# Batch 0's intermediates stored and loaded in three parts of eight instead of two of twelve

## The chip, the cores and the metric

The kernel runs on one core of one Trainium2 chip. The metric is the device time of one execution in microseconds (us). The engines are named as the profile names them: PE is TensorE's matrix multiply and PEld its weight load, DVE is VectorE, ACT is ScalarE, POOL is GpSimd, and SP is SyncE, which here does nothing but issue DMAs. One KB is 1024 bytes; the profile's GB/s are bytes per nanosecond.

## What is computed

Two batches of 3008 tokens with 256 features go through a spectral layer (Fourier transform along the tokens, a complex 256x256 product, a soft threshold, the inverse transform), and the result goes through two MLPs of width 2048. The change touches the spectral layer alone.

```python
X = np.fft.rfft(x, axis=1)                    # x: 2 x 3008 x 256
Yr = Xr @ w_r - Xi @ w_i + b_r
Yi = Xr @ w_i + Xi @ w_r + b_i
Y  = soft_threshold(Yr, 0.01) + 1j * soft_threshold(Yi, 0.01)
y  = np.fft.irfft(Y, n=3008, axis=1)
y  = prelu(y @ w_in1, alpha) @ w_out1         # 256 -> 2048 -> 256
out = g(y @ w_in2) @ w_out2                   # quadratic gate, 256 -> 2048 -> 256
```

## The kernel before

The transform over 3008 tokens is split as 47 x 64. **F1**, the function `f1(g)` (L400 to L421), does the 47-point part for one of 16 groups `g` (0 to 7 are batch 0, 8 to 15 batch 1): four matmuls a half from `xs[g]`, one eviction on ACT and one on DVE into a tile `ae`. Its result has 24 frequencies `k`, each with a real and an imaginary row, along the partitions. The 64-point part needs them along the free side, so the data goes through DRAM: `store_a(k, h)` (L388) writes part `h` of the frequencies of two groups from `ae` to `a_dr[h]`, and `load_a(b, k, n)` (L378) reads frequencies `k` to `k+n-1` of batch `b` back into `a_sb[b]`. Batch 0 has two parts of `N1 = 12` frequencies, batch 1 one part of 24. The columns of the constant `c_f1` put the frequencies of the two parts on every second partition, so that one store takes 48 rows of 8 x 1 KB, 384 KB in all.

**F2** (`f2_parts`, L465) is the 64-point part of one *item*, two frequencies of one batch: item 0 takes frequencies 0 and 1 of batch 0, item 4 takes 8 and 9, item 6 takes 12 and 13, item 12 is the first of batch 1. Its tile on PE is `psf`; it reads `a_sb` (tile `a`) and a table `m`. `mix_sum` and `mix` do the complex product against `wm` (tiles `psk`, `ri`), and `i1` the first inverse part against a table `n` (tile `psi`). The item loop (L733) runs at step `j` F2 of item `j+2`, then `mix_sum` of `j+1`, `mix` of `j`, `i1` of `j-2`. After the spectral layer come the MLPs, which hold PE for the rest of the run.

The order of the work is written out by hand: every engine runs its instructions in the order in which the Python lines stand. The loads of `x` come in `X_CHUNKS`; `X_FULL` names the groups that are loaded as 128 full rows, with their zero rows, in one DMA of 512 KB. The other groups are loaded as 96 rows in two DMAs (64 rows and 32 rows), and their zero rows are written by the `memset` loop at L361, on DVE for groups 3, 5, 7, 9 and on POOL for the rest. A table (L434) says which DMAs SP issues behind which F1 group ("s0" is the store of groups 0 and 1's first part, "w0" the load of `w_r`, "x12" the load of groups 12 and 13, "b0" the bias):

```python
early_loads = {-1: "x0 x1 x2 x4 b0 x6 x8", 1: "s0 x10", 3: "s1", 5: "s2", 7: "s3 w0 w1 x12"}
```

Behind these, SP issues from L452 on: half of table m0, frequencies 0 to 3, x14, the other half of m0, frequencies 4 to 7, n0, frequencies 8 to 11, m1, and the stores of the second part. After F1 of the last groups come two stores of batch 1, the load of frequencies 12 to 23 and tables n1 and m2. A DMA's semaphore is one of eight in turn, so SP also waits, before an issue, for the DMA that was issued eight before it. Between F1 of groups 11 and 12 PE does one bias matmul and four matmuls on a tile of zeros (`warm`, L535) whose result nobody uses.

Of the kernel before, what the change touches and what calls it, by code (L numbers as in the profile page):

```python
# [8 lines left out]
F32 = mybir.dt.float32  # L9
# [7 lines left out]
B, S, D = 2, 3008, 256  # L17
R1, R2 = 47, 64
NK = 24
# [9 lines left out]
X_CHUNKS = [(0, 1), (1, 1), (2, 2), (4, 2), (6, 2), (8, 2), (10, 2), (12, 2), (14, 2)]  # L29
X_FULL = (0, 1)  # L30
N1 = 12
PAIRS = [(0, 512), (1024, 512), (2048, 480)]


def fourier_constants():
# [6 lines left out]
    cs = np.stack([np.cos(a), -np.sin(a)], axis=1)  # L42
    c = np.zeros((2, 64, 4, 64))
    rows = np.array([2 * i if i < 32 else 4 * (i - 32) + 1 for i in range(R1)])
    first, second = (cs[:, :, k].reshape(R1, -1) for k in (slice(0, N1), slice(N1, NK)))
    c[:, rows, 0, 16::2], c[:, rows, 0, 17::2] = first, second
    c[:, rows, 1, 0:48:2], c[:, rows, 1, 1:49:2] = first, second
    c[:, rows, 2, 16:] = c[:, rows, 3, :48] = cs.reshape(R1, 48)
    c = c.reshape(128, 256)

    g = np.zeros((2, 64, 64))
    g[:, 0:96 // 2:2, :R1] = np.cos(a).T
    g[:, 1:96 // 2:2, :R1] = -np.sin(a).T
    g = g.reshape(128, 64)
# [3 lines left out]
    m = np.zeros((NT, 2, 2, NK, 2, R2))  # L58
# [17 lines left out]
    m = m.reshape(8, 2, 2, 2, 2, NK, 2, R2).transpose(0, 1, 4, 2, 3, 5, 6, 7)  # L76
    w = w.reshape(2, R2, NK // 2, 2, 128).transpose(3, 1, 2, 0, 4)
    f = np.float32
# [23 lines left out]
def spectral_mlp_kernel(ctx: ExitStack, tc: tile.TileContext, x, w_r, w_i, bias, c_f1, c_f2,  # L102
# [7 lines left out]
    dram = ctx.enter_context(tc.tile_pool(name="dram", bufs=1, space=DRAM))  # L110
# [31 lines left out]

    a_dr = [dram.tile([8, 4, 2, k, D], F32, name=f"a_dr{k}") for k in (2 * N1, 2 * NK - 2 * N1, 2 * NK)]
    v_dr = [dram.tile([96, NT, D], F32, name=f"v_dr{b}") for b in range(B)]
# [215 lines left out]
    V.memset(warm, 0.0)  # L360
    for g in range(2, 16):  # L361
        (V if g in (3, 5, 7, 9) else G).memset(xs[g], 0.0)
# [15 lines left out]
    def load_a(b, k, n):  # L378
        if a_sb[b] is None:
            a_sb[b] = block(f"a{b}", [128, NK, D], F32, f"a_{b}")  # L380
        h = 2 if b else int(k >= N1)
        src = a_dr[h].rearrange("j w q (z k) f -> (j w q z) k f", z=2)
        k0 = k - N1 * (h == 1)
        nc.sync.dma_start(a_sb[b][:, k:k + n, :], src[:, k0:k0 + n, :])

    A_ROWS = (slice(16, 112, 2), slice(17, 113, 2), slice(16, 112))

    def store_a(k, h, z=None):  # L388
        j = 2 * k % 8
        src, groups = (aes[k], slice(j, j + 2)) if z is None else (aes[k, z], slice(j + z, j + z + 1))  # L390
        dst = a_dr[h][groups].rearrange("j w q i f -> (q i) (j w) f")
        nc.sync.dma_start(dst, src[A_ROWS[h]].rearrange("p g s r f -> p (g s r) f"))

# [39 lines left out]
    wm_src = (w_r, w_i)  # L433
    early_loads = {-1: "x0 x1 x2 x4 b0 x6 x8", 1: "s0 x10", 3: "s1", 5: "s2", 7: "s3 w0 w1 x12"}  # L434

# [21 lines left out]
    load_mn(0, n_t, c_i1)  # L457
    load_a(0, 8, 4)
    load_mn(1, m_t, c_f2)
    for k in range(4):  # L460
        store_a(k, 1)
    conv = conversions(0, list(range(NF)))
    items = [(b, i) for b in range(B) for i in range(NK // 2)]
# [70 lines left out]
    V.tensor_copy(b_t, ri[0])  # L534
    for _ in range(4):  # L535
        T.matmul(ri[1].rearrange("p z e -> p (z e)"), warm[:, 0:128], warm, start=True, stop=True)
# [159 lines left out]
    n = len(items)  # L696
# [28 lines left out]
    for z in range(2):  # L725
        store_a(5, 2, z)
    load_a(0, 12, 12)
    load_mn(1, n_t, c_i1)
    load_mn(2, m_t, c_f2)
    for _ in range(2):  # L730
        next(conv)
    store_a(6, 2)
    for j in range(n):  # L733
# [9 lines left out]
        if j == 3:  # L743
            store_a(7, 2)
            for z in range(2):
                store_a(4, 2, z)
        if j == 6:
# [283 lines left out]
    for i in range(len(seq)):  # L1031
        l, c, f = seq[i]
# [108 lines left out]
```

## Time and profile before

| | before |
|---|---|
| median of 3 runs | 1088.78 us (1088.38 to 1089.55) |
| the profiled execution's own time | 1089.89 us |
| its span, first to last instruction | 1088.1 us |
| PE busy | 1075.9 us, 99% |
| DVE busy | 901.5 us, 83% |
| ACT busy | 815.2 us, 75% |
| moved by DMA | 101.54 MB |

The span is one execution; its own time is 1.8 us more than the span, for what lies around the first and the last instruction. The stretches, waits and timelines used below count from the span's start. A share of busy time is an average over stages: the first 40 us, in which the DMA engines are the busiest part of the core, differ from all that follows, where PE is.

### The profile page before, as it was taken

What the parts mean: (1) busy time and instruction counts of PE and PEld (TensorE: products, weight loads), DVE (VectorE), ACT (ScalarE), POOL (GpSimd) and SP (SyncE); (2) the same over time, 40 slices, a digit from 0 to 9 for tenths busy, and PEclk for the clock granted to TensorE, in tenths of its full rate; (3) what the DMA queues carried; (4) which work ended last, traced back from release to release, by engine and by line L of the source; (5) the groups of instructions that cost most, each with busy time, mean ns of one, the idle gap of its engine ahead of it and who ended that gap; (6) DMA issues with size and microseconds to landing.
All of it is one profiled execution on the core that took longest, in us unless ns stands there. A gap on an engine that the chain in (4) does not pass through costs nothing.

```text
span 1088.1 us, 17038 instructions
## 1 busy us (share of the span) xinstructions
PE 1075.9 (99%) x6376; PEld 940.1 (86%) x6376; DVE 901.5 (83%) x1578; ACT 815.2 (75%) x1497; POOL 45.9 (4%) x46
## 2 busy tenths in 40 slices
PE   7999999999999999999999999999999999999998
PEld 2888888888888998888899988888899888888897
DVE  6788678888879879989989887877878878878876
ACT  4677776656767768888888777778778878877876
POOL 3045400000000000000000000000000000000000
PEclk9999999999999999999999999999999999999999
DMA  9996672001322413315245810010100000100100
GB/s 342 363 316 182 171 162 72 20 20 78 112 105 107 146 43 132 117 60 173 64 134 229 309 40 1 1 39 1 37 3 1 37 1 1 39 1 1 39 1 37
DMA packets 46901, 101.54 MB, mean 93 GB/s; under 512 B 4290, under 2 KB 25922, under 8 KB 45635
## 3 DMA queue, kind: packets, MB, share of 16 engines
q1 hardware_dynamic: 46530, 100.08, 27.3%
q8 instruction: 50, 0.82, 0.3%
q10 hardware_dynamic: 288, 0.39, 0.1%
q14 instruction: 33, 0.26, 0.1%
HBM read 64.92 MB, written 35.52 MB: 92 GB/s over the span
## 4 chain that ended last, share of the span: by engine, by line
PE 83%; ACT 2%; DVE 2%; issue 1%; DVEq 0%; ACTq 0%
PE pq L124 11%; PE pq L125 11%; PE pq L126 11%; PE seeded L124 4%; PE seeded L125 4%; PE seeded L126 4%; PE psh L124 4%; PE pso L124 4%; PE psh L125 4%; PE psh L126 4%; PE pso L125 4%; PE pso L126 4%; PE psA L124 3%; PE psA L125 3%; PE psA L126 3%; PE psC L126 3%
## 5 line engine op out<-in xcount | busy, mean ns | idle before, releaser
L124 PE MATMUL pq<-gh,w 128*128 128x512 f32 (+1 forms) x576 | 216.5, 376 | 0.1
L125 PE MATMUL pq<-gl,w 128*128 128x512 f32 (+1 forms) x576 | 215.9, 375 | 0.1
L126 PE MATMUL pq<-gh,w 128*128 128x512 f32 (+1 forms) x576 | 215.8, 375 | 0.0
L893 ACT ACTIVATE gh<-ta 128x512 fp32r<-128x512 f32 (+1 forms) x144 | 88.1, 620 | 90.8 <-DVE ta L890 84.9
L677 ACT ACTIVATE ta<-psh,slopes 128x512 f32<-128x512 f32 (+1 forms) x96 | 65.2, 679 | 78.7 <-DVE ta L679 42.2
L124 PEld LDWEIGHTS pq<-gh,w 128*128 128x128 f32 x576 | 108.8, 189 | 14.8 <-ACT yt L922 2.1
L125 PEld LDWEIGHTS pq<-gl,w 128*128 128x128 f32 x576 | 108.9, 189 | 13.2 <-DVE gl L896 0.5
L126 PEld LDWEIGHTS pq<-gh,w 128*128 128x128 f32 x576 | 108.9, 189 | 12.9
L896 DVE TENSOR_TENSOR gl<-tb,gh 128x512 fp32r<-128x512 f32 (+1 forms) x96 | 65.3, 681 | 58.5 <-ACT gh L893 58.3
L896 DVE TENSOR_TENSOR gl<-ta,gh 128x512 fp32r<-128x512 f32 (+1 forms) x144 | 97.3, 676 | 2.5 <-ACT gh L893 0.8
L121 DVE TENSOR_TENSOR gl<-ta,gh 128x512 fp32r<-128x512 f32 (+1 forms) x96 | 65.2, 679 | 36.7 <-ACT gh L118 36.4
L981 DVE TENSOR_TENSOR h<-psC,s 128x512 f32<-128x512 f32 (+1 forms) x72 | 48.8, 678 | 40.8 <-PE psC L126 33.1
L124 PE MATMUL psh<-mxh,w 128*128 128x512 f32 (+1 forms) x192 | 72.2, 376 | 0.1
L124 PE MATMUL pso<-gh,w 128*128 128x512 f32 (+1 forms) x192 | 72.3, 377 | 0.0
L125 PE MATMUL pso<-gl,w 128*128 128x512 f32 (+1 forms) x192 | 71.9, 375 | 0.0
L126 PE MATMUL pso<-gh,w 128*128 128x512 f32 (+1 forms) x192 | 71.9, 375 | 0.0
L126 PE MATMUL psh<-mxh,w 128*128 128x512 f32 (+1 forms) x192 | 71.9, 375 | 0.0
L125 PE MATMUL psh<-mxl,w 128*128 128x512 f32 (+1 forms) x192 | 71.9, 375 | 0.0
L679 DVE SCALAR_TENSOR_TENSOR ta<-psh,slopes,ta 128x512 f32<-128x512 f32 (+1 forms) x96 | 70.5, 734 | 0.0
L890 DVE SCALAR_TENSOR_TENSOR tb<-tb,h 128x512 f32<-128x512 f32 (+1 forms) x96 | 60.7, 673 | 0.0
L882 ACT ACTIVATE ta<-ta 128x512 f32<-128x512 f32 (+1 forms) x96 | 59.2, 617 | 1.5
L893 ACT ACTIVATE gh<-tb 128x512 fp32r<-128x512 f32 (+1 forms) x96 | 59.3, 617 | 0.0
(169 smaller groups left out, 2626.9 us busy)
## 6 DMA issues: line engine op xcount, KB each, us to landing
s<-kept SPq DMA_DIRECT2D x32, 512.0 KB, 4.5
u<-in_w_in SPq DMA_DIRECT2D x32, 256.0 KB, 3.0
u<-in_w_out SPq DMA_DIRECT2D x32, 256.0 KB, 3.2
kept<-sh SPq DMA_DIRECT2D x16, 512.0 KB, 3.0
kept<-wh SPq DMA_DIRECT2D x16, 512.0 KB, 2.8
w<-kept SPq DMA_DIRECT2D x16, 512.0 KB, 5.7
v_dr<-ve SPq DMA_DIRECT2D x12, 512.0 KB, 4.6
v<-v_dr SPq DMA_DIRECT2D x32, 192.0 KB, 5.1
```

The lines of the kernel that those rows point to most:

```text
L121: V.tensor_tensor(lo, src, hi.bitcast(F32), op=ALU.subtract)
L124: T.matmul(ps, wl, xh, start=start, stop=False, skip_group_check=chained)
L125: T.matmul(ps, wh, xl, start=False, stop=False, skip_group_check=chained)
L126: T.matmul(ps, wh, xh, start=False, stop=stop, skip_group_check=chained)
L677: A.activation(ta, ps, AF.Copy, scale=slope[:, f:f + 1])
L679: V.scalar_tensor_tensor(ta, ps, sign[:, f:f + 1], ta, op0=ALU.mult, op1=ALU.max)
L882: A.activation(self.t, self.t, AF.Square)
L890: V.scalar_tensor_tensor(self.t, self.t, 1.0, self.h, op0=ALU.min, op1=ALU.max)
L893: A.activation(halves(self.gh, self.m), like_halves(self.t, self.m), AF.Copy)
L896: V.tensor_tensor(halves(self.gl, self.m), like_halves(self.t, self.m), halves(self.gh, self.m).bitcast(F32), op=ALU.subtract)
L981: V.tensor_tensor(blk.h, ps[x], ps[y_], op=ALU.add)
```

## The change

The 24 frequencies of batch 0 go to DRAM in three parts of `NS = 8` instead of two of 12, each on every third partition; a store takes 32 rows and 256 KB. The stores of the first part stay where they were; those of the second stand behind m1 as before, and then comes a load of frequencies 8 to 15 (1024 KB) in place of the load of 8 to 11 (512 KB) that stood ahead of m1. The stores of the third part follow that load, and the load of 16 to 23 (1024 KB) takes the place of that of 12 to 23 (1536 KB). Group 1 of `x` is loaded as 96 rows in two DMAs, and POOL writes its zero rows ahead of the other groups'. The loads of `w_r` and `w_i` move ahead of the stores s1 to s3. PE does three `warm` matmuls instead of four. Indices of batch 1's part go from 2 to 3, and nothing else of it changes.

```diff
-X_FULL = (0, 1)
-N1 = 12
+X_FULL = (0,)
+NS = 8
...
-    first, second = (cs[:, :, k].reshape(R1, -1) for k in (slice(0, N1), slice(N1, NK)))
-    c[:, rows, 0, 16::2], c[:, rows, 0, 17::2] = first, second
-    c[:, rows, 1, 0:48:2], c[:, rows, 1, 1:49:2] = first, second
+    for m in range(3):
+        part = cs[:, :, NS * m:NS * m + NS].reshape(R1, -1)
+        c[:, rows, 0, 16 + m::3] = c[:, rows, 1, m:48:3] = part
...
-    for g in range(2, 16):
+    for g in range(1, 16):
         (V if g in (3, 5, 7, 9) else G).memset(xs[g], 0.0)
...
-    A_ROWS = (slice(16, 112, 2), slice(17, 113, 2), slice(16, 112))
+    A_ROWS = (slice(16, 112, 3), slice(17, 112, 3), slice(18, 112, 3), slice(16, 112))
...
-    early_loads = {-1: "x0 x1 x2 x4 b0 x6 x8", 1: "s0 x10", 3: "s1", 5: "s2", 7: "s3 w0 w1 x12"}
+    early_loads = {-1: "x0 x1 x2 x4 b0 x6 x8", 1: "s0 x10 w0 w1", 3: "s1", 5: "s2", 7: "s3 x12"}
...
     load_mn(0, n_t, c_i1)
-    load_a(0, 8, 4)
     load_mn(1, m_t, c_f2)
     for k in range(4):
         store_a(k, 1)
+    load_a(0, 8, 8)
+    for k in range(4):
+        store_a(k, 2)
...
-    for _ in range(4):
+    for _ in range(3):
         T.matmul(ri[1].rearrange("p z e -> p (z e)"), warm[:, 0:128], warm, start=True, stop=True)
...
-    load_a(0, 12, 12)
+    load_a(0, 16, 8)
```

On SP, from the store s1 to the load of x14, the order before is:

```order
L392 DMA a_dr24_71<-ae1_145 48x8x256
L392 DMA a_dr24_71<-ae2_163 48x8x256
L392 DMA a_dr24_71<-ae3_181 48x8x256
L444 DMA wm32_0_108<-in_w_r 128x512
L444 DMA wm32_1_109<-in_w_i 128x512
L375 DMA x_b_81<-in_x 64x2048
L375 DMA x_b_81<-in_x 32x2048
```

and in the changed kernel, where `a_dr0` is the first part:

```order
L444 DMA wm32_0_110<-in_w_r 128x512
L444 DMA wm32_1_111<-in_w_i 128x512
L392 DMA a_dr0_71<-ae1_150 32x8x256
L392 DMA a_dr0_71<-ae2_168 32x8x256
L392 DMA a_dr0_71<-ae3_186 32x8x256
L375 DMA x_b_82<-in_x 64x2048
L375 DMA x_b_82<-in_x 32x2048
```

The two weight loads pass the three stores, which carry 32 rows instead of 48, and the load x12 stays behind all five.

Further down on SP, from table n0 to the big load, the order before is (`a_dr24_72` is the second part, `a_0` is `a_sb[0]`, `a_dr48` batch 1's part):

```order
L397 DMA n0_105<-in_c_i1 128x1024
L384 DMA a_0_204<-a_dr24_71 128x1024
L397 DMA m1_103<-in_c_f2 128x1024
L392 DMA a_dr24_72<-ae0_125 48x8x256
L392 DMA a_dr24_72<-ae1_145 48x8x256
L392 DMA a_dr24_72<-ae2_163 48x8x256
L392 DMA a_dr24_72<-ae3_181 48x8x256
L392 DMA a_dr48_73<-ae10_240 96x4x256
L392 DMA a_dr48_73<-ae11_249 96x4x256
L384 DMA a_0_204<-a_dr24_72 128x3072
```

and in the changed kernel (`a_dr1` is the second part, `a_dr2` the third):

```order
L397 DMA n0_107<-in_c_i1 128x1024
L397 DMA m1_105<-in_c_f2 128x1024
L392 DMA a_dr1_72<-ae0_128 32x8x256
L392 DMA a_dr1_72<-ae1_150 32x8x256
L392 DMA a_dr1_72<-ae2_168 32x8x256
L392 DMA a_dr1_72<-ae3_186 32x8x256
L384 DMA a_0_207<-a_dr1_72 128x2048
L392 DMA a_dr2_73<-ae0_128 32x8x256
L392 DMA a_dr2_73<-ae1_150 32x8x256
L392 DMA a_dr2_73<-ae2_168 32x8x256
L392 DMA a_dr2_73<-ae3_186 32x8x256
```

The load that holds frequencies 8 to 11, and with them items 4 and 5, now stands directly behind the four stores that it reads, where before it stood behind n0 and read a part that had been stored long before.

## Rows read from the trace of the kernel before

**Rows 1.** The page's first part: busy time and share of each engine.
```profile
PE 1075.9 (99%) x6376; PEld 940.1 (86%) x6376; DVE 901.5 (83%) x1578; ACT 815.2 (75%) x1497; POOL 45.9 (4%) x46
```
**Rows 2.** Waits of PE in the whole span: us in total, times, longest.
```profile
PE ps L416 <- DMA x_a<-in_x: 2.6, 3, 1.1
PE ps L416 <- ACT wm L521: 1.9, 1, 1.9
PE ri L365 <- DVE warm L360: 1.5, 1, 1.5
PE psA L124 <- ACT seeded L970: 0.8, 2, 0.5
```
**Rows 3.** Stretches: busy of PE, PEld, DVE, ACT, POOL; PEclk, DMA share, GB/s.
```profile
10.00:15.00 5.00, 4.52 (x40) 1.54 (x40) 3.77 (x6) 3.16 (x6) 0.00 (x0) 1.00 1.02 367
15.00:20.00 5.00, 4.01 (x33) 1.26 (x26) 2.42 (x4) 2.17 (x4) 0.00 (x0) 1.00 1.03 381
20.00:25.00 5.00, 4.26 (x10) 1.44 (x8) 3.25 (x5) 2.15 (x3) 0.00 (x0) 1.00 0.98 324
25.00:30.00 5.00, 3.85 (x32) 2.46 (x32) 3.65 (x6) 2.75 (x5) 0.00 (x0) 1.00 1.01 403
35.00:40.00 5.00, 5.00 (x46) 4.92 (x45) 4.90 (x14) 2.63 (x7) 0.00 (x0) 1.00 1.03 340
```
**Rows 4.** PE's timeline to 72 us: start, us, [idle before <-releaser].
```profile
1.45 3.56 PE L365 MATMUL ri<-warm 128*128 128x512 f32 x4 [1.45 <-DVE warm L360]
...
20.56 3.70 PE L536 MATMUL ri<-warm 128*128 128x512 f32 x8
26.15 1.95 PE L416 MATMUL ps<-x_b,c 64*64 64x512 f32 x16 [1.90 <-ACT wm L521]
...
38.90 1.06 PE L471 MATMUL psf<-m,a 128*128 128x128 f32 x8
...
47.31 1.16 PE L471 MATMUL psf<-m,a 128*128 128x128 f32 x8
...
55.63 1.16 PE L471 MATMUL psf<-m,a 128*128 128x128 f32 x8
...
72.28 1.16 PE L471 MATMUL psf<-m,a 128*128 128x128 f32 x8
```
**Rows 5.** SP's timeline of DMA issues: start and length of the issue, us.
```profile
0.74 4.31 SPq L375 DMA_DIRECT2D x_a<-in_x  x6
...
15.66 1.98 SPq L444 DMA_DIRECT2D wm<-in_w_r  x1
17.69 1.25 SPq L444 DMA_DIRECT2D wm<-in_w_i  x1
19.03 1.16 SPq L375 DMA_DIRECT2D x_b<-in_x  x2
...
26.03 0.33 SPq L384 DMA_DIRECT2D a<-a_dr  x1
26.65 0.33 SPq L397 DMA_DIRECT2D m<-in_c_f  x1
...
39.79 0.34 SPq L384 DMA_DIRECT2D a<-a_dr  x1
```
**Rows 6.** Issue to landing of x12's second DMA, issued at 19.59 us.
```profile
x_b<-in_x SPq DMA_DIRECT2D x1, 256.0 KB, 6.4
```
**Rows 7.** The same of table m1, issued at 26.65 us.
```profile
m<-in_c_f SPq DMA_DIRECT2D x1, 512.0 KB, 9.0
```
**Rows 8.** The same of the second part's last store, issued at 30.49 us.
```profile
a_dr<-ae SPq DMA_DIRECT2D x1, 384.0 KB, 9.2
```
**Rows 9.** The same of the load of frequencies 12 to 23, issued at 39.79 us.
```profile
a<-a_dr SPq DMA_DIRECT2D x1, 1536.0 KB, 7.1
```
**Rows 10.** SP's own waits, 0 to 60 us: the longest.
```profile
SPq L384 <- DMA a_dr<-ae: 3.0, 1, 3.0
```
**Rows 11.** Loads of 512 KB from DRAM with little else moving, from 440 us on.
```profile
DMA to landing us min/median/max: 3.2/4.8/8.3
```
**Rows 12.** Stretches around PE's last matmul, columns as in rows 3.
```profile
1084.30:1086.69 2.39, 0.00 (x0) 0.00 (x0) 0.00 (x0) 0.57 (x1) 0.00 (x0) 1.00 0.94 354
1086.70:1088.10 1.40, 0.00 (x0) 0.00 (x0) 0.00 (x0) 0.00 (x0) 0.00 (x0) 0.50 0.00 0
```
**Rows 13.** Batch 1's first load, issued at 62.81 us, to landing.
```profile
a<-a_dr SPq DMA_DIRECT2D x1, 1024.0 KB, 6.4
```
**Rows 14.** POOL's timeline, first 10 us.
```profile
0.73 5.39 POOL L362 MEMSET x_a<- 128x1024 f32 x6 [0.29 <-POOLq L1129]
```
**Rows 15.** The first two loads of x, issued from 0.74 us on, to landing.
```profile
x_a<-in_x SPq DMA_DIRECT2D x2, 512.0 KB, 4.6
```

More of the change, by code (lines that the diff above doesn't have):

```diff
@@ L141, in piece @@
         return p[:, 112:112 + 768]
-    a_dr = [dram.tile([8, 4, 2, k, D], F32, name=f"a_dr{k}") for k in (2 * N1, 2 * NK - 2 * N1, 2 * NK)]
+    a_dr = [dram.tile([8, 4, 2, k, D], F32, name=f"a_dr{n}") for n, k in enumerate((2 * NS, 2 * NS, 2 * NS, 2 * NK))]
     v_dr = [dram.tile([96, NT, D], F32, name=f"v_dr{b}") for b in range(B)]
@@ L380, in load_a @@
             a_sb[b] = block(f"a{b}", [128, NK, D], F32, f"a_{b}")
-        h = 2 if b else int(k >= N1)
+        h = 3 if b else k // NS
         src = a_dr[h].rearrange("j w q (z k) f -> (j w q z) k f", z=2)
-        k0 = k - N1 * (h == 1)
+        k0 = k if b else k - NS * h
         nc.sync.dma_start(a_sb[b][:, k:k + n, :], src[:, k0:k0 + n, :])
-    A_ROWS = (slice(16, 112, 2), slice(17, 113, 2), slice(16, 112))
+    A_ROWS = (slice(16, 112, 3), slice(17, 112, 3), slice(18, 112, 3), slice(16, 112))
     def store_a(k, h, z=None):
@@ L725, in spectral_mlp_kernel @@
     for z in range(2):
-        store_a(5, 2, z)
-    load_a(0, 12, 12)
+        store_a(5, 3, z)
+    load_a(0, 16, 8)
     load_mn(1, n_t, c_i1)
@@ L731, in spectral_mlp_kernel @@
         next(conv)
-    store_a(6, 2)
+    store_a(6, 3)
     for j in range(n):
@@ L743, in spectral_mlp_kernel @@
         if j == 3:
-            store_a(7, 2)
+            store_a(7, 3)
             for z in range(2):
-                store_a(4, 2, z)
+                store_a(4, 3, z)
         if j == 6:
```

## The prediction

> **What bounds the kernel now.** I read the page's busy times first [rows 1]: PE is busy for 1075.9 of 1088.1 us, so only the other 12 us, or work taken off PE, can change the time. The list of PE's waits [rows 2] says where they lie: the long ones are on L416, F1's matmuls, and on L365, the first warm-up, all in the first 27 us; the largest later one is 0.8 us in two pieces. The change touches nothing of the MLPs. So the question is at what time PE gets through the start, and any shift there moves the end one for one as long as no later load becomes late.
>
> The stretches [rows 3] say what sets the start. From 10 to 40 us the DMA engines' share is 0.98 to 1.03: the queue is full, and a load lands when the bytes ahead of it have moved. They move at 367, 381, 324 and 403 GB/s in the four 5-us stretches from 10 to 30. PE's longest wait is the 1.90 us before 26.15 [rows 4]. The row names an ACT instruction, but the second DMA of x12 is issued at 19.59, lands 6.4 us later [rows 6], at 26.0, and that is what group 12 needs. From 35 us on PE has no gap, and DVE is nearly full too (4.90 of 5.00).
>
> **Part 1: how much earlier PE could be.** The bytes ahead of x12 fall by 128 KB (group 1) and 4 x 128 KB (the first part's stores), 640 KB or 0.655 MB; at the 353 GB/s of 15 to 25 us that is 1.9 us, so 24.1 instead of 26.0. More may come: in 20 to 25 us the rate dips to 324 GB/s, and x12's issue stands behind the issues of the two weight loads, which took 1.98 and 1.25 us [rows 5] where each of the first six took about 0.6. The weights now pass the stores, so x12 is issued earlier. If the dip goes, 5 us x 79/403 = 1.0 us more is won; I take half, x12 at 23.6. PE itself is free for group 12 at 20.56 + 3.70 = 24.26 before. One warm-up matmul of four goes (3.70/4 = 0.93 us), and x10, with 256 KB less ahead of it, comes 0.7 us earlier: 22.6. The later of the two, 23.6, holds; the range is 23.1 to 24.1, a gain of 2.0 to 3.0 us, and I take 2.5. The weights' earlier landing takes a wait off ACT and DVE, which stays hidden behind x12. So PE would reach F2 of item 4, at 38.90 before [rows 4], at 36.4.
>
> **Part 2: what the new second part costs.** Before, items 4 and 5 read a load that was issued at 26.03 [rows 5], ahead of m1, from data stored long before. Now they read a load that SP may issue only when the four stores before it have landed. The trace has the same pattern one part later: SP waits 3.0 us for such stores [rows 10] before it issues the load of 12 to 23 at 39.79 [rows 5]. There nobody waited: issued at 39.79, it landed 7.1 us later, at 46.9 [rows 9], and item 6 came at 47.31 [rows 4]. I build the new time from these rows:
>
> - Table m1 lands at 26.65 + 9.0 = 35.65 before [rows 7]. Ahead of it go 128 + 512 KB as above and the 512 KB of the old load, 1152 KB or 1.18 MB; at the mean of 369 GB/s that is 3.2 us, and half the dip another 0.5: 31.95.
> - The four stores: the last landed at 30.49 + 9.2 = 39.7 [rows 8], 4.0 us after m1, for 1536 KB. For 1024 KB that is 2.7 us: 34.65. SP issues the load 0.1 us later, at 34.75.
> - The load of 1024 KB starts with an empty queue, since all else stands behind it on SP: the third part's stores, batch 1's, the load of 16 to 23, n1, m2 and the first MLP weights. From below: 512 KB took 3.2 us at the least [rows 11], and another 512 KB at 400 GB/s take 1.3: 4.5 us. From above: the load of 1536 KB took 7.1 us [rows 9] with two stores still ahead of it; less 512 KB, 5.8. I take 4.9, nearer the lower end, because this queue is empty. It lands at 39.65.
>
> Item 4 thus starts at 39.65 instead of 38.90: **0.75 us later than before**, after a stall of 39.65 - 36.4 = 3.25 us in which PE has nothing else, because its order is fixed. All that part 1 wins is lost in it. With 5.8 us and no dip won back it is 41.05 (+2.15); with 4.5 and all of the dip, 38.75 (-0.15).
>
> The Trainium skill, "DMA: Bandwidth & Descriptors", section "Anatomy of one DMA", gives a fixed cost of some 2.0 us and the bytes at 436 GB/s, most of the fixed part being the receipt of the last write; it is measured for another issue path. For 512 KB it gives 3.2 us, the row's smallest; for this load 4.4, an estimate, and the sum below would be 0.5 us smaller.
>
> **Part 3: the clock.** A stall of 3.25 us is longer than any in the trace before. The one longer idle stretch is at the end [rows 12]: the granted clock is still 1.00 in the 2.39 us after PE's last matmul, then 0.50, which is 1.2 GHz. After 1.90 us idle at 26.15 it was 1.00. So I expect it to fall in this stall. What a return costs is read at the start [rows 4]: two warm-up matmuls took 3.56 us there and four took 3.70 later, so those two lost 3.56 - 1.85 = 1.7 us, at about half the later pace, which I take for the lower clock. Bounds: 0 if the clock holds, 1.7 if it falls; I take 1.7, since 3.25 us is well above 2.39. PE is dense behind the stall, so this isn't regained.
>
> **Part 4: edits that cost nothing.** Group 1's zero rows are one more memset on POOL, 5.39/6 = 0.9 us [rows 14], ahead of all its others. x1's load waits for it, until 0.73 + 0.9 = 1.63, instead of following x0's issue at once, and has one issue more (4.31/6, waits included, 0.7 us at most) [rows 5]. What hides it: the first two loads of x took 4.6 us to land [rows 15], so x0's bytes are in the queue for some two more us; uncovered it would be about 1.2 us. POOL's later memsets slip by 0.9 us and lead the loads that need them. The third part's stores and the load of 16 to 23 take a second trip, which at part 2's lengths ends some 10 us behind the first, at about 50; item 8, which needs it, is at 55.63 [rows 4]. Later DMAs keep their order.
>
> A rule of the skill speaks against the two DMAs: "DMA: Bandwidth & Descriptors", section "Rules for kernel authors", says two transfers to disjoint partitions serialize, and to use one over 128 partitions. By it the extra issue is pure cost, here 0.7 us if it showed.
>
> **The sum.** 0.75 + 1.7 = 2.45 us. On the profiled execution's 1089.89 that is 1092.3. It lies 1.1 us over the median of the runs, so for the median, 1088.78 + 2.45 = **1091.2 us**. A measurement of this kernel can tell about 0.2%, 2.2 us, from no change, so the forecast is slower by an amount at that edge.
>
> **The rivals.**
>
> 1. *The stall comes, the clock holds.* For it: nothing in the trace shows the clock fall inside the run, and the end's stretch differs in that PE did nothing more at all. Against it: 2.39 us sufficed there. Then 1088.78 + 0.75 = 1089.5, with the bounds of part 2 1088.6 to 1090.9.
> 2. *The second part lands in time, not slower than before.* Decides at 36.4: if the load lands by then, part 1's gain stands, 1088.78 - 2.5 = 1086.3, and in between each us earlier is a us. For it: the dips in the DMA rate may all go. Against it: the bytes ahead and the two trips through DRAM give 38.75 at the best of my bounds. 1086.3 to 1088.6.
> 3. *A second load turns late.* Batch 1's first load lands at 62.81 + 6.4 = 69.2 [rows 13] and item 12 needs it at 72.28 [rows 4], 3.1 us of room. SP now waits empty-handed twice instead of once, and the new hole is the load's 4.9 us less the 2.6 us of its bytes, 2.3 us, against 0.3 us of bytes saved. If that and slower 1 KB rows put the queue more than 3.1 us behind PE, a second stall follows: 1093 to 1095.
>
> **How the numbers follow.** Stall and clock fall: 0.55, with a range of 1089.6 to 1093.0 from part 2's bounds and a partial loss of clock; a little over half of it lies more than 0.2% above. Rival 1: 0.25. Rival 2: 0.10, of which a third is more than 0.2% faster. Rival 3: 0.10, all slower. So slower: 0.30 + 0.10 + 0.03 of rival 1's upper end = 0.43; faster 0.04; the same 0.53. The likeliest case has its middle just past the 0.2%, which is why its time stands beside a larger chance for no change. The range from 1088.2 to 1093.0 holds the forecast's case and rival 1, and leaves out most of rivals 2 and 3.
>
> **What would show it.** In PE's waits: the 1.9 us before group 12 mostly gone, group 12 at about 23.6, and a new wait of about 3 us on L473's `psf` for a load of `a`. On SP: the wait at the load of 8 to 15 until about 34.7, and that load landing near 39.7. In the stretches: PEclk under 1.00 between 37 and 43 us, and items farther apart there. Wrong if `psf` shows no wait (part 2), if the clock stays at 1.00 (part 3), or if item 12 waits (rival 3).

## The result and the profile after

The changed kernel takes **1095.72 us** (median of 5 runs, 1094.46 to 1097.22) against 1088.78 (1088.38 to 1090.31) for the kernel before: a ratio of 1.0060, with a 95% interval of 1.0049 to 1.0072. The forecast was 1091.2, with a range up to 1093.0. The direction and the mechanism came as forecast; the size is almost three times as large.

The profiled execution took 1097.22 us, the longest of the five, with a span of 1095.4 us, 7.3 more than before. A second measurement of the same file further down (`e11_after_again`) gave 1094.72 us, and its profiled execution took 1094.49. I use both traces wherever a size matters. PE's busy time in the first, from the page, against [rows 1]:

```profile
PE 1077.7 (98%) x6374; PEld 942.2 (86%) x6374; DVE 901.3 (82%) x1578; ACT 815.6 (74%) x1497; POOL 46.8 (4%) x47
```

Two matmul records less (the warm-up matmul that went) and yet 1.8 us more busy time; the rows below show work that ran at a lower clock. The other 5.5 us of the span are waiting. PE's waits in the first 60 us (us in total, times, longest), which answer to [rows 2]:

```profile
PE psf L473 <- issue: 6.3, 1, 6.3
PE ps L416 <- DMA x_a<-in_x: 3.5, 2, 2.9
PE ri L365 <- DVE warm L360: 1.5, 1, 1.5
PE ps L416 <- DMA x_b<-in_x: 0.5, 1, 0.5
PE psf L473 <- DMA a<-a_dr: 0.5, 1, 0.5
```

The wait of 1.9 us on L416 for group 12 is gone, and a wait of 6.3 us on L473's `psf` is new. Its releaser reads "issue", but the load of frequencies 8 to 15 lands at 44.42 and the matmul starts at 44.51: it is that load. PE's timeline (start, us, idle before), which answers to [rows 4]:

```profile
10.10 7.86 PE L416 MATMUL ps<-x_a,c 64*64 64x512 f32 x64 [2.88 <-DMA x_a<-in_x]
...
24.29 1.95 PE L416 MATMUL ps<-x_b,c 64*64 64x512 f32 x16
...
44.51 2.04 PE L473 MATMUL psf<-m,a 128*128 128x128 f32 x8 [6.33 <-issue]
...
51.17 1.16 PE L473 MATMUL psf<-m,a 128*128 128x128 f32 x8
...
55.33 1.16 PE L473 MATMUL psf<-m,a 128*128 128x128 f32 x8
```

The row at 24.29 is group 12, without a wait; that at 44.51 is item 4, which stood at 38.90 before: 5.61 us later. Item 5 follows after 6.66 us; before it followed after 4.25 (from 38.90 to 43.15), so another 2.41 us are lost between the two. From item 6 on, every item is 8.0 us late and the distance is the 4.16 us of before; some 0.7 us come back later, 0.44 of them a wait ahead of L649 near 140 us that is not there in this trace. That leaves the 7.3 us of the span.

The stretches around the stall (columns as in [rows 3]):

```profile
38.18:42.98 4.80, 0.00 (x0) 0.00 (x0) 1.90 (x4) 0.90 (x2) 0.00 (x0) 1.00 0.95 301
42.98:44.51 1.53, 0.00 (x1) 0.03 (x1) 0.00 (x0) 0.00 (x0) 0.00 (x0) 0.50 1.04 331
44.51:49.81 5.30, 5.30 (x25) 5.30 (x26) 1.94 (x4) 1.29 (x3) 0.00 (x0) 0.50 0.85 255
```

PE is idle from 38.18. The granted clock is 1.00 until 42.98, then 0.50, which is 1.2 GHz, to 49.81; 5.30 us of that PE spends on dense work. So both halves of the forecast's 2.45 us exist: the stall at item 4, and the clock behind it. In the repeat item 4 starts at 42.00 after a wait of 4.21, and item 5 follows 5.77 later:

```profile
42.00 1.69 PE L473 MATMUL psf<-m,a 128*128 128x128 f32 x8 [4.21 <-issue]
47.77 1.16 PE L473 MATMUL psf<-m,a 128*128 128x128 f32 x8
```

Item 4 is 3.10 us later than before there, and the clock costs 1.52. The two traces differ in item 4's start by 2.5 us (the load is issued 1.2 us earlier in the repeat and takes 1.3 us less), and in how long the lower clock lasts, 6.83 us and 3.41. The mean granted clock of each of the ten executions of this kernel is 0.996 to 0.998; the repeat's traced one, with its 3.41 us at 0.50, has 0.998, so the clock fell in all ten. In nine executions of the kernel before (`e10_before_again`) it is 0.999 or 1.000, which the lower clock behind PE's last matmul [rows 12] explains.

### The profile page after: what moved, and what is told of

Same layout as the page of the kernel before. It is cut to its first block, busy times and chain, and to the rows that moved or that the text cites. A ratio compares the mean times of both kernels' runs of the same rounds, so it can differ in the third digit from the quotient of the medians.

```text
span 1095.4 us, 17049 instructions
## 1 busy us (share of the span) xinstructions
PE 1077.7 (98%) x6374; PEld 942.2 (86%) x6374; DVE 901.3 (82%) x1578; ACT 815.6 (74%) x1497; POOL 46.8 (4%) x47
## 4 chain that ended last, share of the span: by engine, by line
PE 82%; ACT 2%; DVE 2%; issue 0%; DVEq 0%; ACTq 0%
PE pq L124 11%; PE pq L125 11%; PE pq L126 11%; PE seeded L124 4%; PE seeded L125 4%; PE seeded L126 4%; PE psh L124 4%; PE pso L124 4%; PE psh L126 4%; PE psh L125 4%; PE pso L126 4%; PE pso L125 4%; PE psA L124 3%; PE psA L126 3%; PE psA L125 3%; PE psC L126 3%
```

## The experiments

All kernels stand against the kernel before, run on the same chip, which had medians of 1089.00 to 1089.18 us.

| kernel | what it is | median, us | ratio to before, 95% | item 4 starts |
|---|---|---|---|---|
| `e1_no_trip` | after, load of 8 to 15 needs no new store | 1089.30 | 0.9999 (0.9991 to 1.0008) | 38.82 |
| `e2_stores_early` | after, second part's stores ahead of n0, m1 | 1092.88 | 1.0033 (1.0021 to 1.0044) | 40.47 |
| `e3_rest_alone` | before, with all but the three parts | 1089.84 | 1.0005 (0.9997 to 1.0014) | 38.53 |
| `e4_x1_full` | after, x1 in one load of 128 rows | 1094.31 | 1.0043 (1.0031 to 1.0055) | 41.95 |
| `e5_keep_warm` | after, PE kept busy in the stall | 1093.05 | 1.0032 (1.0020 to 1.0045) | 41.52 |
| `e6_load_2_and_6` | after, load of 8 to 15 as 2 + 6 | 1093.11 | 1.0035 (1.0022 to 1.0047) | 38.85 |
| `e7_rest_load_4_and_8` | e3, load of 12 to 23 as 4 + 8 | 1089.04 | 1.0001 (0.9992 to 1.0010) | 39.70 |
| `e8_early_full_2_6` | e2, e4 and e6 together | 1090.07 | 1.0004 (0.9995 to 1.0014) | 38.30 |
| `e9_batch1_load_2_6` | e8, batch 1's first load as 2 + 6 | 1089.17 | 1.0000 (0.9991 to 1.0008) | 37.40 |
| `e10_before_again` | the kernel before | 1088.99 | 1.0000 (0.9990 to 1.0010) | 37.85 |
| `e11_after_again` | the changed kernel | 1094.72 | 1.0055 (1.0043 to 1.0068) | 42.00 |
| `e12_x1_alone` | before, with x1 in two DMAs | 1089.51 | 1.0003 (0.9995 to 1.0012) | 38.36 |
| `e13_weights_alone` | before, with the weights' loads moved | 1089.62 | 1.0005 (0.9996 to 1.0015) | 38.12 |
| `e14_weights_back` | after, weights' loads back | 1095.36 | 1.0061 (1.0048 to 1.0073) | 41.91 |
| `e15_load_behind_x14` | after, load of 0 to 3 behind x14 | 1091.52 | 1.0021 (1.0012 to 1.0030) | 40.87 |
| `e16_all_and_weights_back` | e9, weights' loads back | 1088.76 | 0.9999 (0.9991 to 1.0008) | 37.01 |

Item 4's start is from one trace each, and traces of one file differ: the kernel before shows 38.90 and 37.85, the changed one 44.51 and 42.00. A trace is also of one execution out of five to twelve, and not always of a typical one: those of e2 and e5 are from the fastest execution, those of e6 and e8 from the slowest. Where a time and a trace disagree, I go by the time.

### Is it the trip through DRAM?

**e1_no_trip** lets the load of 8 to 15 read the first part, stored long before:

```diff
-        h = 3 if b else k // NS
+        h = 3 if b else (0 if k == 8 else k // NS)
...
-        k0 = k if b else k - NS * h
+        k0 = k if b else (0 if k == 8 else k - NS * h)
```

> The changed kernel, but the load of frequencies 8 to 15 reads the first part again instead of the second, so it need not wait for the four stores ahead of it. (Frequencies 8 to 15 of batch 0 then hold the wrong values; sizes, order and bytes are the same.) Theory A, the trip: the loss is PE's wait at F2 of item 4 for store, landing, issue and load. Then the load follows the stores in a full queue and lands near 39 to 40 us instead of 44.4; the stall falls from 6.3 to under 2 us, the clock holds, and the time is 1087 to 1090 us. Theory B, the start: the loss comes from x1 in two DMAs behind a POOL memset and from a queue that moves fewer bytes in the first 30 us; then the load still lands after 42 us and the time stays over 1093.

1089.30 us: the whole loss is gone. SP issues the load at 28.89 instead of 37.34 (the changed kernel's row first, then e1's), and PE's rows at items 4 and 5 are:

```profile
37.34 0.33 SPq L384 DMA_DIRECT2D a<-a_dr  x1
28.89 1.47 SPq L384 DMA_DIRECT2D a<-a_dr  x1
...
38.82 1.13 PE L473 MATMUL psf<-m,a 128*128 128x128 f32 x8 [1.68 <-issue]
42.96 1.16 PE L473 MATMUL psf<-m,a 128*128 128x128 f32 x8
```

Everything else of the change is in this kernel, so the order store, landing, issue, load is the cause of the loss, clock included. The remaining wait of 1.68 us also says that taking the trip away alone does not bring item 4 ahead of its old place, 38.90 and 37.85: the load, now without a wait, takes 9.8 us and lands at 38.73, with the loads and stores issued before it still in the queue.

**e2_stores_early** shortens the same path in another way:

```diff
-    load_mn(0, n_t, c_i1)
-    load_mn(1, m_t, c_f2)
     for k in range(4):
         store_a(k, 1)
+    load_mn(0, n_t, c_i1)
+    load_mn(1, m_t, c_f2)
     load_a(0, 8, 8)
```

> The changed kernel, with the four stores of the second part ahead of the tables n0 and m1 instead of behind them, so that 1024 KB of table loads move while the stores land. Theory A: the load of 8 to 15 is issued with the tables still in the queue and lands some 3 us behind m1, at 38.5 to 40 us; F2 of item 4 stalls 1 to 2 us, the clock holds, and the time is 1087.5 to 1090. Theory B: the start is as late as in the changed kernel; the time is 1092 or more.

1092.88 us. The load is issued at 33.58 and lands at 40.33; item 4 waits 2.95 us, and the granted clock stays at 1.00 in this trace. It is the trace of the fastest of six executions, 1091.36 us; the mean granted clock of the other five is 0.996 to 0.998, so there it fell. The expectation's theory A, 1087.5 to 1090, missed. Of the loss, clock included, 1.8 to 2.8 us go with the two tables that no longer stand ahead of the stores, and the rest stays.

### What the clock costs

**e5_keep_warm** fills the stall with 22 matmuls whose result nobody uses:

```diff
     for j in range(n):
+        if j == 2:
+            busy = psum.tile([128, 2, D], F32, tag="e", name="busy")
+            for _ in range(22):
+                T.matmul(busy.rearrange("p z e -> p (z e)"), wm[0][:, 0, 0, 0:128],
...
```

> The changed kernel with 22 matmuls of 512 columns on data at hand, their result unused, put on PE directly ahead of F2 of item 4, so that PE works for some 4.7 us of the stall. The load that item 4 waits for is as late as ever. Theory C, the clock is a part of its own: the granted clock stays at 1.00, items 4 and 5 are 4.2 us apart instead of the 6.7 in the changed kernel, and the time falls by 1.5 to 2.5 us, to 1093.2 to 1094.2. Theory A alone, all of the loss is the late load: the slow clock is hidden behind ACT and DVE, and the time stays at 1095 to 1096.5.

1093.05 us, 1.7 below the repeat of the changed kernel and 2.7 below its first measurement. PE's rows around item 4:

```profile
36.50 5.18 PE L739 MATMUL busy<-wm 128*128 128x512 f32 x22
41.52 1.05 PE L473 MATMUL psf<-m,a 128*128 128x128 f32 x8
...
45.57 1.16 PE L473 MATMUL psf<-m,a 128*128 128x128 f32 x8
```

Item 4 is 2.62 us later than in the kernel before, item 5 follows after 4.05 us, and the granted clock is 1.00 throughout. This execution took 1091.55 us, 2.4 above the median of the kernel before on that chip (1089.12): the late item 4 alone. The load landed at 40.58, so the added matmuls outlast it by 0.9 us here, and by this trace the gain of 1.7 to 2.7 us understates what the clock costs. It is also the fastest of five executions; the mean granted clock is 1.000 in four of them, and these four took 1091.55 to 1094.65 us, so with the clock held the time is still 2.4 to 5.5 us over the kernel before. The clock is a part of its own, about 2 us by the medians and 1.52 and 2.41 us by the changed kernel's traces, and the stall is the larger part.

### The other edits alone

**e3_rest_alone** puts everything but the three parts into the kernel before (`X_FULL = (0,)`, the memset from group 1 on, the weights' loads in row 1, three warm-up matmuls, `N1 = 12` kept), and **e12_x1_alone** only the first two of these:

```diff
-X_FULL = (0, 1)
+X_FULL = (0,)
...
-    for g in range(2, 16):
+    for g in range(1, 16):
         (V if g in (3, 5, 7, 9) else G).memset(xs[g], 0.0)
```

> The kernel before, with two parts of twelve, and the rest of the change: x1 as 96 rows with its zero rows written on POOL, the weights' loads ahead of the stores, three warm-up matmuls. Theory A: nothing waits at item 4; item 4 starts 0.5 to 1.5 us earlier than before, and the time is 1087.3 to 1088.8, unless item 6 now waits for the load of 12 to 23, which had 0.4 us of room. Theory B: the start itself is worse, and the time is 1090 or more.

> The kernel before with one edit: x1 as 96 rows in two DMAs, its zero rows written on POOL ahead of the other groups'. If the edit is free, as the prediction has it, the 128 KB less bring x2 and x12 0.3 us earlier and the time is 1088.3 to 1089.3. If the wait for the memset and the extra issue thin the queue out at the start, x2 lands 0.5 to 1.5 us later than before and the time is 1089.5 to 1090.5.

Neither moves the time measurably. e3's 1089.84 lies between its two theories. In its trace item 6 has the wait that theory A allowed for, for the load of 12 to 23, where the kernel before has none in one trace and 0.21 us in the other:

```profile
48.34 1.13 PE L471 MATMUL psf<-m,a 128*128 128x128 f32 x8 [1.32 <-DMA a<-a_dr]
```

**e7_rest_load_4_and_8** splits that load, and the wait is gone, again without a difference in time that can be told:

```diff
-    load_a(0, 12, 12)
+    load_a(0, 12, 4)
+    load_a(0, 16, 8)
```

> The kernel before with the rest of the change (as e3), and the load of 12 to 23 cut into one of 12 to 15 and one of 16 to 23. e3 was 1089.8 us with one wait of 1.3 us at item 6, whose load landed at 48.2. If that wait is all that keeps it over the kernel before: the wait goes, since the first 512 KB land some 2.5 us earlier, and the time is 1088.0 to 1088.8. If the rest of the change costs at the start as well (x1 behind its memset), the time stays at 1089.3 to 1090.

**e4_x1_full** takes x1's part out of the changed kernel (`X_FULL = (0, 1)`, the memset from group 2 on):

> The changed kernel with x1 loaded as 128 full rows again, without its POOL memset. Theory A: item 4 waits for the same trip, and the time is that of the changed kernel, 1094.5 to 1097. Theory B: the 2.9 us that PE waited for x2 in the changed kernel fall to about 1.1 as before, the queue runs 1 to 2 us earlier, and the time is 1092.5 to 1094.

1094.31 us; the interval overlaps that of the changed kernel's two measurements, so the time doesn't show it. The stretch from 5 to 10 us does. The changed kernel, and then e4 (GB/s at the end):

```profile
5.00:10.00 5.00, 2.22 (x17) 0.54 (x16) 2.21 (x4) 1.20 (x2) 5.00 (x7) 1.00 0.89 304
```

```profile
5.00:10.00 5.00, 2.87 (x24) 0.83 (x28) 2.20 (x4) 1.20 (x2) 4.67 (x6) 1.00 1.02 406
```

In the eleven traces with x1 in two DMAs the rate of this stretch is 304 to 386 GB/s, with a mean of 354; in the seven with one DMA it is 404 to 423, mean 414. 60 GB/s for 5 us are 0.30 MB, and the edit saves 0.13 MB. So by the rows it costs the queue about 0.17 MB, some 0.5 us by this estimate, which is less than a time measurement shows. The edit is the second DMA and the wait for POOL's memset together; no run separates the two.

### Does a second load turn late?

**e6_load_2_and_6** gives item 4 its two frequencies first:

```diff
-    load_a(0, 8, 8)
+    load_a(0, 8, 2)
+    load_a(0, 10, 6)
```

> The changed kernel with the load of frequencies 8 to 15 cut into one of 8 and 9 (256 KB, all that item 4 needs) and one of 10 to 15 (768 KB). If the trip's price is mainly bytes, item 4 starts 2 us earlier and more (1.9 us of bytes, and fewer packets for a late DMA engine to be behind with): stall 3.5 to 4.5 us, time 1091.5 to 1094. If it is mainly the fixed part, the landing of the stores, the issue and the way to the first packet, item 4 starts less than 1 us earlier and the time stays over 1094.5.

The small load takes 3.1 us, from 35.66 to 38.76, and item 4 starts at 38.85 after 2.0 us, yet the time is 1093.11. PE's waits from 55 to 80 us in its trace:

```profile
PE psf L474 <- DVE fl L495: 1.8, 1, 1.8
PE psf L474 <- ACT u L178: 1.3, 1, 1.3
```

Both are new. Up to item 8, at 55.51 (55.63 and 54.84 in the two traces of the kernel before), this trace loses little: its loss, in the slowest of the five executions (1094.70), arises behind that, and with it comes the lower clock, from 61.99 us on. Item 9, at 61.53, waits for DVE, which had itself waited for the first MLP weights (landed at 57.55), and item 12, at 77.00, waits for batch 1's first load, which lands at 76.87; the page names the engines that come between. The reading is that with the first stall short PE arrives where the queue isn't yet. It is not the stall's length alone: in the traces of e1, e2 and e15, with stalls of 1.68, 2.95 and 1.57 us at item 4, no item behind has such a wait. **e8_early_full_2_6** (the edits of e2, e4 and e6) does away with the first stall:

> The changed kernel with three edits: the second part's stores ahead of n0 and m1 (e2), x1 as 128 full rows (e4), and the load of 8 to 15 cut into 8, 9 and 10 to 15 (e6). Theory A says that only the trip stands between the change and its gain: the first 256 KB land 0.7 to 2 us behind m1, at 36 to 38, where PE is ready at 36.6 to 38; item 4 waits under 1 us and starts 1 to 2 us earlier than before. The time is 1087 to 1088.3. If x12 and the loads behind it are late in their own right, it is 1089 or more.

1090.07 us, above the 1087 to 1088.3 of the expectation's theory A. Item 4 has no wait; in its trace, from the slowest of eleven executions (1092.94), item 12 has one, and the lower clock follows. The mean granted clock is 0.998 in this and two more executions (1091.60 to 1092.94) and 1.000 in the other eight (1087.94 to 1090.85), so this second stall with its lower clock is not the rule:

```profile
73.71 1.43 PE L474 MATMUL psf<-m,a 128*128 128x128 f32 x8 [1.95 <-DMA a<-a_dr]
```

```profile
74.39:77.80 3.41, 3.41 (x19) 3.41 (x18) 1.34 (x3) 1.16 (x3) 2.34 (x3) 0.50 1.04 415
```

**e9_batch1_load_2_6** splits batch 1's load too:

```diff
-            load_a(1, 0, 8)
+            load_a(1, 0, 2)
+            load_a(1, 2, 6)
```

> e8 with batch 1's first load cut into 2 frequencies (256 KB, all that item 12 needs) and 6. In e8's trace item 4 no longer waits, but item 12 waits 1.9 us for that load and the clock falls. If the late queue shows there alone, item 12 waits less than 0.5 us, the clock holds and the time is 1088 to 1089.2, at or under the kernel before. If the queue is late for the first MLP weights and the other loads as well, other waits take its place and the time stays at 1089.5 to 1091.

The only wait of an item from 28 to 80 us that is left is 0.2 us; item 0, at 26.19, waits 0.93 us. The time is 1089.17: equal to the kernel before.

### Why the queue moved less from 20 to 30 us

**e10_before_again** and **e11_after_again** are the two kernels once more, for a second trace of each.

> The kernel before once more, for a second trace of it. If what moved in its first 30 us (324 GB/s from 20 to 25 us, then 403; x2 landing at 8.3, m1 at 35.7) is what that order gives, the second trace shows it within 0.5 us. If it is chance, x2's and m1's landings differ by 1 us or more, and item 4 with them. The time is 1088 to 1090.

> The changed kernel once more, for a second trace. The first was of its longest execution, 1097.2 us, with x2 landing at 10.0, m1 at 34.5 and the load of 8 to 15 taking 7.1 us. If the long stall is what the order gives, the second has again a stall of 4.5 us or more at item 4, the clock at 0.50 behind it and a load of over 6 us. If the load's length was one late DMA engine, it is 4.8 to 5.5 us here and the stall shorter. The time is 1094 to 1097.

They show that m1's landing was missed in both traces of the changed kernel, at 34.48 and 33.39 instead of 31.95, and why becomes visible on SP. The stretches of the changed kernel from 20 to 30 us, first and second trace, against the 324 and 403 GB/s of [rows 3]:

```profile
20.00:25.00 5.00, 5.00 (x24) 1.71 (x20) 3.94 (x6) 3.04 (x5) 0.00 (x0) 1.00 0.93 352
25.00:30.00 5.00, 4.48 (x40) 2.61 (x36) 4.50 (x9) 3.66 (x8) 0.00 (x0) 1.00 0.92 279
...
20.00:25.00 5.00, 4.19 (x16) 1.48 (x18) 4.11 (x7) 3.16 (x4) 0.00 (x0) 1.00 1.02 306
25.00:30.00 5.00, 4.32 (x40) 2.58 (x36) 3.42 (x7) 2.75 (x6) 0.00 (x0) 1.00 0.94 360
```

SP's timeline of issues in that place, first trace (start, us, out<-in):

```profile
17.40 1.41 SPq L375 DMA_DIRECT2D x_b<-in_x  x2
18.86 0.59 SPq L397 DMA_DIRECT2D m<-in_c_f  x1
21.85 0.34 SPq L384 DMA_DIRECT2D a<-a_dr  x1
22.28 2.12 SPq L375 DMA_DIRECT2D x_b<-in_x  x2
```

From 19.45 to 21.85 us SP issues nothing. The row at 21.85 is the load of frequencies 0 to 3; it reads what s0 to s3 store, and s3 lands at 21.77. The weights' loads, now ahead of s1 to s3, push these stores back in the queue, and x14 and all behind it waits on SP with the load. Two things make the 2.4 us: the store lands 1.2 us later than before (20.55), and SP, done with its issues sooner, is at the load 1.4 us earlier (20.82 before).

**e13_weights_alone** makes that one move in the kernel before, **e14_weights_back** takes it out of the changed kernel:

```diff
-    early_loads = {-1: "x0 x1 x2 x4 b0 x6 x8", 1: "s0 x10 w0 w1", 3: "s1", 5: "s2", 7: "s3 x12"}
+    early_loads = {-1: "x0 x1 x2 x4 b0 x6 x8", 1: "s0 x10", 3: "s1", 5: "s2", 7: "s3 w0 w1 x12"}
```

> The kernel before with one edit: the loads of w_r and w_i ahead of the stores s1 to s3. In the changed kernel SP stands 1.3 to 2.4 us in front of the load of frequencies 0 to 3, which reads the last of these stores (issue of m0's half ends at 19.45, that load is issued at 21.85 when the store has landed at 21.77), and everything behind it on SP slips. Theory W (the moved weights make this wait, since the three stores now land behind them): it is here too, over 1 us of SP's waiting between 19 and 24 us, and the DMA engines move less than 335 GB/s from 20 to 30 us, where the kernel before had 363 to 374. Item 4 needs a load that was issued long before, so the time stays at 1088.5 to 1090. Rival R (the smaller rows of the three parts, or x1's two DMAs, lower the rate): no wait there, and 360 GB/s or more.

> The changed kernel with the loads of w_r and w_i back behind the stores s1 to s3. Theory W: no wait at the load of frequencies 0 to 3, 355 GB/s or more from 20 to 30 us, m1 lands at 32.5 or earlier (33.4 and 34.5 in the changed kernel's two traces), the load of 8 to 15 is issued by 35.2, item 4 starts at 39.8 to 41.0, and the time is 1092 to 1093.5: slower than before by the rest of the stall. Rival R: as the changed kernel, m1 at 33.4 or later, 1094 to 1096.

e13, SP's wait between 17 and 24 us, and its stretches:

```profile
SPq L384 <- DMA a_dr<-ae: 2.6, 1, 2.6
```

```profile
20.00:25.00 5.00, 4.00 (x9) 1.44 (x8) 4.01 (x7) 2.99 (x3) 0.00 (x0) 1.00 0.92 311
25.00:30.00 5.00, 4.26 (x36) 2.70 (x40) 3.15 (x6) 2.54 (x6) 0.00 (x0) 1.00 1.01 346
```

e14, the stretches; the load of 0 to 3 is issued at 19.51 there, right behind m0:

```profile
20.00:25.00 5.00, 4.36 (x20) 1.65 (x22) 4.11 (x7) 3.23 (x4) 0.00 (x0) 1.00 0.98 330
25.00:30.00 5.00, 4.75 (x43) 2.38 (x34) 4.09 (x8) 3.30 (x8) 0.00 (x0) 1.00 1.01 406
```

The wait comes with the move and goes with it. The same over all traces: the mean rate from 20 to 30 us is 313 to 350 GB/s in the twelve with the weights ahead and the load at its place, and 363 to 382 in the five with the weights behind. That much is shown. What e14 was to show beyond it did not come: m1 landed at 33.05, not by 32.5, item 4 started at 41.91 after 4.74 us, and the time is 1095.36, no better than the changed kernel. So the missing rate goes with part of m1's lateness, and giving it back in this way does not give back the time.

**e15_load_behind_x14** leaves the weights and moves the load that waits:

```diff
-    load_a(0, 0, 4)
     load_x(14)
     load_mn(0, m_t, c_f2, 1)
+    load_a(0, 0, 4)
     load_a(0, 4, 4)
```

> The changed kernel with the load of frequencies 0 to 3 two places later, behind x14 and m0's second half; the weights stay ahead of the stores. Theory W: the same wait for the last store is short or gone at the load's new place, x14 and m0 go into the queue 1 to 2 us earlier, m1 lands at 32.5 or earlier, item 4 starts at 40 to 41, 1091.5 to 1093.5. Rival R: m1 at 33.4 or later, 1094 to 1096.

1091.52 us, 3.2 and 4.2 below the changed kernel's two measurements. m1 lands at 32.01, the last store at 34.65, the load is issued at 34.78. PE's waits from 28 to 80 us, and the rows at items 4 and 5:

```profile
PE psf L473 <- DMA a<-a_dr: 2.4, 1, 2.4
PE psf L473 <- issue: 1.6, 1, 1.6
```

```profile
40.87 1.13 PE L473 MATMUL psf<-m,a 128*128 128x128 f32 x8 [1.57 <-issue]
45.00 1.16 PE L473 MATMUL psf<-m,a 128*128 128x128 f32 x8
```

In the trace the gain has two sources. Item 4 starts at 40.87, 1.1 and 3.6 us earlier than in the two traces of the changed kernel. And the idle time is now in two pieces, 2.4 us at item 0, which gets its load later, and 1.6 at item 4; the granted clock stays at 1.00 and item 5 follows after 4.13 us. The second source is not shown for the time: the mean granted clock is 0.998 or less in seven of the eleven executions, so in these it fell, and they took 1090.99 to 1092.45 us, hardly longer than the other four with 1091.03 to 1092.27. Where in them it fell, and how the 3.2 to 4.2 us divide, stays open.

**e16_all_and_weights_back** is e9 with the weights' loads behind the stores:

> The changed kernel with the four stores of the second part ahead of n0 and m1, x1 loaded full, the load of 8 to 15 and batch 1's first load each as 2 + 6 (all as in the kernel that measured 1089.17), and the loads of w_r and w_i back behind the stores s1 to s3. Theory W: the queue doesn't run low from 20 to 30 us, so item 4 needs no wait and starts at or before 37.4, item 12 doesn't wait, and the time is 1087.5 to 1088.8: a little below the kernel before at best. Against it: x12 lands later again, and PE's wait ahead of group 12 comes back with 1 to 2 us, which puts item 4 at 38 and the time at 1089 to 1090.

PE's waits from 28 to 80 us:

```profile
PE psi L583 <- DMA n<-in_c_i: 0.8, 1, 0.8
PE psk L512 <- ACT ae_a L417: 0.3, 1, 0.3
PE psf L474 <- DMA a<-a_dr: 0.2, 1, 0.2
```

1088.76 us against 1089.18 of the kernel before on the same chip, with an interval of 0.9991 to 1.0008. With PE's waits from 28 to 80 us down to 1.3 us in all, three parts are worth what two were. No kernel here beats the kernel before by more than the measurement can tell.

## Why the prediction was right or wrong

- **What is slow, and where: right.** The stall at item 4 on L473's `psf`, SP's wait ahead of the load, PE's wait ahead of group 12 mostly gone: all as forecast, and e1 shows that the trip is the cause.
- **Part 1, x12 right, item 4's earliest time wrong.** x12 landed at 23.62 and 24.00, forecast 23.6. But PE itself was free for group 12 only at 24.29 (at 23.33 in the repeat), not at 22.6. The term that fell is the 0.7 us by which x10 was to come earlier: it landed at 18.45 and 17.43, against 17.49 before. In the first trace PE had also waited 2.88 us for x2, before 10.10. PE was ready for item 4 at 38.18 and 37.79, not at 36.4. I subtracted a gain from the 38.90 of a single trace; the second trace of the kernel before has item 4 at 37.85, so a good part of that gain was the spread between executions. The second trace's row:

```profile
37.85 1.06 PE L471 MATMUL psf<-m,a 128*128 128x128 f32 x8
```

- **Part 2, m1's landing: the first failed size.** 31.95 forecast, 34.48 and 33.39 measured, issued at 26.02 and landed 8.5 us later in the first trace:

```profile
m<-in_c_f SPq DMA_DIRECT2D x1, 512.0 KB, 8.5
```

  The step that fell is the half of the dip taken as won back, and with it the rate at which the bytes were priced: I took the weights' move for a cure of the dip in 20 to 25 us, and it held SP up at the load of 0 to 3, for 2.4 us in the one trace and 1.3 in the other, and the dip lasted to 30 us. From 20 to 30 us the queue moved 3.15 and 3.33 MB, against 3.63 before; at the forecast's 369 GB/s the missing bytes are 1.3 and 0.8 us, and with the 0.5 us taken for the dip that makes 1.8 and 1.3 us of the 2.5 and 1.4 that m1 was late, an estimate. I had read the order on SP for what passes what, and not for which load reads the stores that were pushed back. e15, where that load stands behind x14, has m1 at 32.01, the last store at 34.65 and the issue at 34.78: forecast 31.95, 34.65 and 34.75 for another order, so such times can be reached, and the agreement to 0.1 us is luck. e14, which removes the wait the other way, reached 33.05 only: its rates from 10 to 20 us are 370 and 372 GB/s, where e15 has 405 and 398, and why is open.
- **Part 2, the stores: right.** The last one landed 2.74 and 2.64 us behind m1; forecast 2.7.
- **Part 2, the load: the second failed size.** 4.9 us with a bound of 5.8; measured 7.08 and 5.76. The same load of 1024 KB into an emptied queue took 6.04 us in e4, 5.13 in e5, 6.00 in e14 and 6.00 in e15: a median of 6.0 over the six traces. (In e2 it took 6.75, but there the tables n0 and m1 were still ahead of it; m1 landed at 36.05.) "This queue is empty" pulled my value to the lower end, and the bound from a whole load, 5.8 us, was the nearer one, though its row [rows 9] had two stores still ahead. The lower end stood on the smallest of [rows 11]; their median, 4.8, with the same 1.3 us on top gives 6.1, and [rows 13] has a load of the same 1024 KB at 6.4. Issue to landing of the changed kernel's load:

```profile
a<-a_dr SPq DMA_DIRECT2D x1, 1024.0 KB, 7.1
```

  The Trainium skill, "DMA: Bandwidth & Descriptors", section "Anatomy of one DMA", gives 2.0 us and the bytes at 436 GB/s, an estimate of 4.4 us here. No trace agrees, the nearest being 5.1; its fit is for another issue path.
- **Part 3, the clock: right in what came, not in its ground.** Forecast 1.7 us; 2.41, above its upper bound, and 1.52 in the two traces, and about 2 in e5's time. That it falls I took from 3.25 us being above 2.39, and the rows at the end of this document do not bear that comparison out: it fell after 1.82 and 1.95 us, and not after 2.95. Rival 1, in which it holds, is what the traces of e5 and e15 look like, but at 1093.05 and 1091.52 us, over its 1090.9, because the stall is longer than forecast.
- **Part 4: nearly right.** x1's two DMAs and the moved weights cost nothing measurable alone (e12, e13). But that they cost nothing was wrong of the queue: the one loses some 60 GB/s in 5 to 10 us, the other some 40 from 20 to 30. Neither shows in the kernel before, where the load that items 4 and 5 need is issued long ahead. Both are ahead of the trip in the changed one, yet undoing one of them there (e4, e14) brings no time that can be told; only e15 does, which moves the load that waits. The Trainium skill's rule in "DMA: Bandwidth & Descriptors", section "Rules for kernel authors", is that two transfers to disjoint partition halves only serialize. The trace does not speak against it, with 354 against 414 GB/s, but the wait for the memset is in that number too.
- **Rival 2, in time: refused.** Even without the trip (e1) the load lands at 38.73, 1.6 us after PE is ready (37.14).
- **Rival 3, a second late load: not in the changed kernel, but real.** No item behind item 4 waits there; that the long stall gave the queue its time is argued, not shown. In two of the kernels that cut the stall short it comes up, in e6 at 61.53 and 77.00 and in e8 at 73.71, and in the traces of e1, e2 and e15 it does not.
- **The sum.** 0.75 + 1.7 = 2.45 us became 5.61 + 2.41 in one trace and 3.10 + 1.52 in the other. The stall's term was mis-sized by 2.4 to 4.9 us, by m1 (1.4 to 2.5) and the load (0.9 to 2.2). Taken against the second trace of the kernel before, the repeat's 3.10 is 4.15, and 4.15 + 1.52 = 5.67 us is close to what the medians on that chip differ by, 5.69. The chance of 0.43 for slower was too small for the same reason: the range's upper bound was built with m1 at 32.45 at the latest and a load of 5.8 us at the longest.

## What to carry to other kernels

When a load is put behind the store that it reads, the path is the sum of everything that lands before the store, the store's own landing and a whole issue-to-landing of the load; price the last with a whole load seen in the trace, not with the smallest one plus bytes. When DMAs are reordered on one queue, look for the load that reads what was pushed back: it stops the issuing engine, and with it everything that is queued behind. And a saving in front of a resource that stays nearly full (here the DMA engines in the first 80 us) bought nothing that could be measured, even with PE's visible waits nearly gone (e9, e16).

## What the runs showed of the hardware

- The same load of 1024 KB took 5.1 to 7.1 us from issue to landing in six traces of five kernels that differ little, always with the queue emptied before it. In the longest, the first trace of the changed kernel, fifteen of the sixteen counts that its semaphore gets had come by 42.67 us and the last came at 44.42: one late part made 1.75 of the 7.08 us.
- The granted clock fell after idle stretches of PE that were shorter than some after which it did not fall: after 1.82 us before 61.53 in e6 (0.50 from 61.99 on) and 1.95 us before 73.71 in e8 (0.50 from 74.39 on, above), when PE was at work again; it stayed at 1.00 after 2.95 us in e2's trace and 1.90 us in the kernel before [rows 4]. Nor does the kernel alone decide: of six executions of e2 it held in the traced one and fell in the other five (mean granted clock 1.000 against 0.996 to 0.998). The 2.39 us at the end of the run, from which I had forecast the fall, were no measure for it; by what rule it falls, these rows don't say. The stretch of e2's stall:

```profile
37.52:40.47 2.95, 0.00 (x1) 0.03 (x1) 1.90 (x4) 0.90 (x2) 0.00 (x0) 1.00 0.97 331
```
